# A cross network on one core: a new table of row products, from a planner whose model has the ring's banks, the kernel's order of reads, close input tiles and longer phases

## The chip, the cores and the metric

The kernel runs on one NeuronCore of a Trainium2 chip. The metric is the device time of one execution, in microseconds. Five engines take part, each with a queue of its own that it works through in order: PE (TensorE, the matmuls, with its weight loads shown as PEld), ACT (ScalarE), DVE (VectorE), POOL (GpSimd) and SP (SyncE, which here only issues DMAs). They wait for each other through semaphores. PSUM, into which PE writes, has eight banks of 512 columns; one bank holds one result of 128 features by 512 batch rows.

## The reference: what is computed

Six cross layers over a batch of 16384 rows with 416 features, in bfloat16:

```python
x = x0
for l in range(6):
    proj = x @ ws[l] + bs[l]        # [16384, 416] x [416, 416]
    x = x0 * proj + x
```

Layer l+1 needs the whole feature vector of layer l, but only of its own batch rows, so different parts of the batch are independent of each other.

## The kernel before, in words

**Tiling.** The batch is cut into 8 groups of 2048 rows; a pair (g, l) is a job, group g at layer l, and there are 48 jobs. x lies transposed in SBUF, features on partitions. The 416 features make three full tiles of 128 (NT = 3) and a tail of 32. A group has 4 chunks of 512 columns (NJ = 4). The tails of the four chunks lie stacked in one 128-partition tile, 32 partitions each (`x3s`), so that chunk j of a job has its tail in row quarter `quad(g, l, j)`.

For one chunk of one output tile of a job, PE must add 13 products of 32 contraction rows: each of the three full tiles gives four (one for each 32-row quarter of the array), and the tail gives one, on the row quarter in which it lies. A "row product" is a 32x128 weight against a 32x512 moving operand, placed at one of the array's four row groups. The four row groups run side by side, each into a different PSUM bank; two row groups must not write the same bank at the same time.

**Order of the jobs.** Jobs run along diagonals of (group, layer) (`order`), so that a job's input was made by a job a few places earlier. The output tiles of most jobs form one list of chunks, 504 of them, from tile 1 of job (0, 2) to tile 0 of job (7, 4): the stream (`stream`). The 32-feature output tails of the jobs are computed apart from it, in 14 phases that fall between chunks, each for three jobs (`tails`). A phase uses column groups of the array instead of row groups: 36 products of 128x32 (L694) and 12 of 32x32 (L682) into three banks.

**The table.** The order of the row products on PE is written out by hand in the string `ORDER`, the result of a search outside of the kernel. Each letter is a visit of one row to one chunk: with k the letter's place in the alphabet `LETTERS`, the row is k mod 4 and the chunk is the one begun k div 4 chunks before the next new one; k div 4 = 0 (A to D) begins the next chunk. A visit issues all that this row has to do for this chunk: three products, and a fourth on the row that holds the tail (for the last four chunks of the stream, the tail's product alone). A bar `|` is a phase. There are 2018 visits and 14 bars.

**The planner.** `replay` walks the table and gives every product a time on a clock of its own, 20 units (`SLOT`) to a product. That clock decides three things and then is gone: the order in which the products of the four rows are interleaved in PE's single queue (`out.sort`), the PSUM bank of each chunk (the bank that comes free first on that clock), and, through `read`, when DVE's work for a chunk is put behind a phase's own DVE work (`behind_tail`). In the clock:

- a row that goes to a chunk another row has just left waits `FENCE` units after that row's last product;
- when all four rows are done with a chunk, ACT reads its bank `READ` units later, ACT takes `NEXT` units a read, and the bank is free `BACK` units after the read's start (`over`);
- a phase of m jobs takes all rows off for 65 m + 27 units and uses three free banks;
- at the stream's start, banks 0 to 3 are free, 4 and 5 come free at 92, 6 and 7 at 186, and ACT is busy until 170.

The chip takes no notice of this clock. On the chip PE issues the products in program order and stops at the first one whose bank has not been read by ACT or whose input has not been written by DVE.

**After PE.** When a chunk's 13th product is issued in the program, `evacuate_chunk` adds ACT's eviction with the bias (L547, PSUM to `tw`), and for each pair of chunks of a tile DVE's multiplication with x0 (L559) and the addition of x (L564), which writes the tile that the next layer reads. The eviction frees the bank. ACT evicts in the order in which the last products are issued. The phases' results go through ACT (L605) or DVE (L601), and DVE (L607, L609); in some jobs SP then rotates the stacked tail by whole quarters with two DMAs (L441, L442).

**Before and after the stream** whole tiles are computed with 128-row matmuls (L647, L635, L668), and their banks come from `ring`, a list of the eight bank numbers from which `take` removes the first n and puts them at the end. The tile just before the stream is tile 0 of job (0, 2); ACT evicts it with two reads of 1024 columns (L511). After the stream, `ring` is set from the banks that are left.

**SP's queue** holds the loads of the groups in the order in which the program adds them: `start_job` adds the load of a group's x0 when the first product of a certain job is added (that of group 4 with job (2, 1), whose first chunk is number 56 of the stream), and `tails` adds rotations and outputs when a phase is added.

Of the kernel before, what the change touches and what calls it, by code (L numbers as in the profile page):

```python
# [21 lines left out]
class Program:  # L22
# [175 lines left out]


SLOT = 20  # L200
FENCE, CHANGE = 22, 9
READ, NEXT, BACK, SECOND, PAIR, TAILS = 19, 56, 70, 92, 56, 220
LETTERS = "ABCDEFGHIJKLMNOPQRSTUVWXYZabcdefghijklmnopqrstuvwxyz0123456789"
ORDER = (
    "ABCDABaXOTUBCjUReLMhSHIVOTYBOIDhKAbJCQLVOEBXOQDNKADZOQXBOIDVCfMJSXYFOIDVCMXdSIHB|CXMRCPIBaDUZKTA"
    "JaTMVCLUBSXANSLUdCLMVTCNISDYJSPEBCTAZSPUJGDQVCTIBaTJAKDcZWTAJOTUZKHQBCXQNKDIZSDQJCTANSbAZSLUBKTU"
    "NCLAZWTMBKPcVSDIR|CTJUCTIVODANaTUJGDAZSXINCLUBSXANSLgVGPAVODUNKDUJCXIRCDUNSbAJCTUZLMeRXCINSDYJSP"
    "EBCTAZSPUJGDQVCTANaTUJCDUZOTEBaPURCLQNCbMBWPIZSDIR|CTJUCTIVCDUNaTIBaTVAKTNUGDMVSDINCXANCbVgSLENW"
    "DUNCPUJSDIRObEBCTUBSPAZCTUZKDUJaDIRWPEZKTMBKDRcLCIRCnJQCDMVaTIFWPQBCTMVCPAZWPIBWDUNCPcVKTEZOXANW"
    "QBP|QBOLRECTBCUPZSAPRaXASJPUBKUPRCAPRWYDSJMXCJUDSJMXGBAbWdAXORLUCJTUOBLUCVTMCJDQaVLMCXBQOXJEaBDU"  # L210
    "OZTEKVDUKTBQKNDICbRICTBYSPBMaLVAKTVAKPQVGDcNWDUN|ICXJTACVQPCNAPeVAPeRYLWNQDKNbCIBWTYBSLMVCLMVCXM"
    "JSDIZSPFACTUBSPIVCDYVOTANaTAZKTUNGDNUSDJAXCMVSDgJSbUFLOAVDOQVCPQJCfIRODJAaDMVKDcJSbAJTOYVGDMVCjU"
    "N|ISDJTAKRATBODUeNTYGVATVOIDJWAXRKDYBWPQBObRCQDdOQLVaMDWJMTCJAfSVIDSJUDRKUPFCMDBaQfVKALRWMDJOUDV"
    "CMTBOYjREWDRWMLBUKDVISNXACBSYXJOEDaVDQBSbcJOXEZCXM|RCPISFDAWTcBKTMVGDUNSDMJTCIBSXIdOHQBPCMVDOAZW"
    "PBUOLAVCfURCTcJWPQZCPIRWDJQWPEBCTAZSPUJCLAZCXMRaLUBWLAVLSgNXGIRCDUNS|IDJTECRODANCfYVKTMFWDUNCPAN"
    "aXJQODdATOJUCLUBSXANKDYVCPQhaXFICXRYCPIRWDJQWDAVOTBMKbAVCPcRWLYFCXQZCPIRWDJQWPEBCTAZSPUJCLAZCXMR"
    "aLUBWLAVLSgNXGIRCDUNS|IDJTECRODANCfYVKTMFWDUNCPANaXJQODdATOJUCLURODINCbUBWTMJCLAZWTANSLUBDSUhLYN"
    "GXIRCTBMSBPIaRDICTVICBXcaRPEWDNQWLBQKDZICbRAaTJUOHBMWRDICXRYKPBAaPRWAPRKUDJCYTCNYDWZMLeBUbKRMHWB"
    "MXRCM|RCPISFDAWDMVKTYFCDYROfIFCXQZKDRIeDQJPGABfQVKHMBWPAOVAPKVADNWTYJGDYBWTMZKXEBWDQVOLAVKTAJSAD"
    "OVYDNKYTBKbMVSHBeMXRCM|RCPISFDQCDMVaTIBSbUBTKMVCLMVSDIBSXIZDKURDSMJCbIBSXIZOHQBCTMVCPIVSDQJCTIBa"  # L220
    "DUZSLAJbQOVHAOBbUOBLUChTIVOALVOQDJCXQBiLMSVDKMBbWJMHCVASXdIDJSUPCJUDSVIDSBMbRCYLRCQbJWALVMSDJMaD"
    "JYOXRAO|ANXKQBLSABOXYRGLMVDWNACbNAaXNSDYNSDYJCTUCfVISbENWLBUSDAVOTYJGDQVODINDCNYXSEBSjMVGLQBSDMR"
    "KDAdOXBUOLAVCfURCTcJWPQZCPIRWDJQWPEBCTAZSPUJCLAZCXMRaLUBWLAVLSgNXGIRCDUNS|IDJTAKRMDJCQbJWATVCQPJ"
    "WALBaUTBODUadTIGVATVOIDJWAXRKYPFCMDBaMTCZAPVaIDJSAfRKUPFCMXBWgLROEDNmAXJOQDJCQXKxEPBWMDNWAPVKAXB"
    "OQDNaAPZKcTFODMZWDUJOfAVK|MBXKNALWNQCDNQCbJAWTBQePVGbARWPYCPJUSFDQCTIZCTANaDYVKPQFWDAVMKbRUTBSNM"
    "CD"
)


def replay(tails, events, keep, part):  # L230

    n = len(tails)
    size = [[(3 if c < n - keep else part) + (r == tails[c]) for r in range(4)] for c in range(n)]
    free, flight, begun, act = [0] * 4, {}, 0, 170
    banks = [(0, 0), (0, 1), (0, 2), (0, 3), (92, 4), (92, 5), (186, 6), (186, 7)]
    home, read, out, latest, due = {}, {}, [], [[]] * 4, list(events)

    def over(now):
        nonlocal act
        for end, c in sorted((end, c) for c, (left, end, q) in flight.items() if not left and end <= now):
            del flight[c]  # L250
            if c < n - keep:
                start = max(act, end + READ)
                act, read[c] = start + NEXT, start + BACK
                banks.append((start + BACK, home[c]))
        banks.sort()

    for letter in ORDER:
        if letter == "|":
            now, m = min(free), due.pop(0)
            parts = [(f - now) // SLOT for f in free]  # L260
            at = now + max((f - now) % SLOT for f in free)
            over(at)
            on = at + 65 * m + 3 * CHANGE
            moved = [on + SLOT * k for k in parts]
            for f in flight.values():
                f[1] = moved[f[2]] if f[1] == free[f[2]] else -9 * SLOT
            got = [banks.pop(0) for _ in range(m)]
            assert all(t <= at + 3 * SLOT * k for k, (t, _) in enumerate(got))
            for r in range(4):
                for k in range(parts[r]):  # L270
                    latest[r][-1 - k][0] = moved[r] - SLOT * (k + 1)
            for k, (_, b) in enumerate(got):
                if k == 1:
                    banks.append((on + SECOND, b))
                    continue
                start = max(act, on - CHANGE + READ)
                act = start + NEXT
                banks.append((start + BACK, b))
            banks.sort()
            free = moved  # L280
            out.append([at, -1, [b for _, b in got], on])
            continue
        age, r = divmod(LETTERS.index(letter), 4)
        c, now = begun - age, free[r]
        over(now)
        if not age:
            t, home[c] = banks.pop(0)
            start, begun = max(now, t), begun + 1
            flight[c] = [sum(1 << q for q in range(4) if size[c][q]), 0, r]
        else:  # L290
            start = max(now, flight[c][1] + FENCE)
        assert flight[c][0] >> r & 1
        free[r] = start + SLOT * size[c][r]
        flight[c] = [flight[c][0] & ~(1 << r), free[r], r]
        latest[r] = [[start + SLOT * k, r, c, home[c]] for k in range(size[c][r])]
        out += latest[r]
    over(max(free))
    assert begun == n and not flight and not due
    out.sort(key=lambda x: (x[0], x[1]))
    return out, read, [b for t, b in banks]  # L300


def bass_standalone__cross_network_dcn__recsys_kernel(
# [8 lines left out]
    NT = 3  # L312
    NJ = 4
# [61 lines left out]
    ring = list(range(8))  # L375
# [56 lines left out]
    def turn_of(g, l):  # L432
        return (0, 1, 1, 2)[g % 4] if l % 2 else 0

    def quad(g, l, j):
        q = (j + turn_of(g, l)) % NJ
        return q, slice(q * T32, (q + 1) * T32)
# [417 lines left out]
    def job_banks():  # L855
        return take(NJ)
# [3 lines left out]
    x0n7, x5n, on = (x0s[s][:, 0:XW + CH].rearrange(view, j=NJ, k=KK) for s in (sn, s5, so))  # L860
# [75 lines left out]
    tiles = [((1, 0), 0), ((1, 0), 1), ((0, 1), 0), ((0, 1), 1), ((0, 1), 2), ((1, 0), 2)]  # L936
# [12 lines left out]
    k = 0  # L949
# [52 lines left out]
    def stream(run, keep, part):  # L1002

        chunks = [(it[1], it[2], j) for it in run if it[0] == "tile" for j in range(NJ)]
        due, n = [], 0
        for it in run:
            if it[0] == "tails":
                due.append((n, it[1]))
            else:
                n += NJ  # L1010
        plan, read, left = replay([quad(g, l, j)[0] for (g, l), i, j in chunks], [len(b) for n, b in due],
                                  keep, part)
        phases.extend(on for _, r, _, on in plan if r < 0)
        count, seen = {}, {}
        for _, r, c, b in plan:
# [8 lines left out]
            q, ecols = slice(r * T32, (r + 1) * T32), slice(i * P, (i + 1) * P)  # L1024
            t = seen[c, r] = seen.get((c, r), -1) + 1
# [16 lines left out]
        banks = [home[c] for c in range(len(chunks) - keep, len(chunks))]  # L1042
# [25 lines left out]
    for n, it in enumerate(items):  # L1068
        if n == s_lo:
            stream(items[s_lo:s_hi], NJ, 0)  # L1070
# [15 lines left out]
        elif mode[n] in ("FR", "F1"):  # L1086
            banks = job_banks()
# [3 lines left out]
        else:  # L1091
            banks = job_banks()
# [13 lines left out]
    g, l = LAST, L - 1  # L1106
# [113 lines left out]
    for kk in range(1, KK):  # L1220
        begun = (1,) if kk == 1 else ()
# [47 lines left out]
```

## Time and profile before

| | us |
|---|---|
| median of 3 runs | 470.0 (469.94 to 470.43) |
| the profiled execution, whole | 470.27 |
| its span, first to last instruction | 468.5 |
| PE busy | 460.2 |
| DVE busy | 402.9 |
| ACT busy | 379.1 |
| the stream, first row product to the next full product after it | 40.86 to 432.34 |
| first column product of the phases 1, 2, 3 | 56.11, 81.65, 106.66 |
| the same of the phases 13 and 14 | 387.40, 416.39 |

The granted TensorE clock is full (0.999). In a row of the cost groups stand the line of the code, the engine, what is written and read, the shape, the count, the busy time and the mean duration of one in ns, and after the second bar the time that the engine stood idle just before such instructions and what ended it. A matmul's duration reaches to the end of its way through the array, so that matmuls that follow each other overlap; how fast they follow is read from their starts. In the chain, consecutive pieces of one kind are joined, with their number behind an x. In a line of waits stand the waiting engine with its line, what it waited for, the total in us, the number of times and the longest.

### The profile page before, as it was taken

How to read it: one execution, taken by the hardware profiler on the slowest of the kernel's cores; microseconds unless marked ns; L12 is line 12 of the kernel's file. 1: busy time of each engine (PE TensorE's matmuls, PEld its weight loads, DVE VectorE, ACT ScalarE, POOL GpSimd, SP SyncE). 2: the span in 40 equal slices, each digit the busy share in tenths (PEclk: the TensorE clock that was granted, in tenths of full speed). 3: DMA queues.
4: the chain of work that ended last, by engine and by line, in shares of the span. 5: the costliest groups of instructions: out<-in, count | busy, mean ns of one | idle time of the engine just before them, and what ended most of it. 6: DMA issues, size and time to landing. Idle time of an engine off the chain costs nothing.

```text
span 468.5 us, 17458 instructions
## 1 busy us (share of the span) xinstructions
PE 460.2 (98%) x7827; PEld 259.6 (55%) x7833; DVE 402.9 (86%) x700; ACT 379.1 (81%) x605; POOL 7.6 (2%) x15
## 2 busy tenths in 40 slices
PE   9999999999999999999999999999999999999995
PEld 5344555565556666575555556565576564545442
DVE  1897898898899898989899899898989889789897
ACT  4686898888888798888878888888887888878685
POOL 1000000000000000000000000000000010000000
PEclk9999999999999999999999999999999999999999
DMA  8986750480002879094848447990100195025999
GB/s 221 191 150 138 169 122 13 81 138 25 3 3 36 149 202 160 26 148 148 160 81 146 148 82 137 160 298 19 25 2 6 35 159 158 3 46 108 240 192 261
DMA packets 139087, 53.77 MB, mean 115 GB/s; under 512 B 112762, under 2 KB 138500, under 8 KB 139012
## 3 DMA queue, kind: packets, MB, share of 16 engines
q1 hardware_dynamic: 138856, 52.54, 53.5%
q8 instruction: 61, 1.00, 0.9%
q10 hardware_dynamic: 156, 0.11, 0.1%
q14 instruction: 14, 0.11, 0.1%
HBM read 5.97 MB, written 13.63 MB: 42 GB/s over the span
## 4 chain that ended last, share of the span: by engine, by line
PE 94%; DVE 3%; DMA 1%; ACT 1%; issue 0%; DVEq 0%; ACTq 0%
PE ps L1030 69%; PE ps L694 7%; PE ps L1034 6%; PE ps L647 6%; PE ps L635 2%; PE ps L682 1%; DMA x<-x 1%; DVE x L1184 1%; PE ps L768 1%; PE ps L668 1%; DVE x L1178 1%; PE ps L786 1%; ACT tw L511 1%; DVE x L525 0%; DVE tw L520 0%
## 5 line engine op out<-in xcount | busy, mean ns | idle before, releaser
L1030 PE MATMUL ps<-x,wm 32*128 32x512 bf16 x6000 | 357.0, 374 | 1.5 <-DVE x L564 1.0
L547 ACT ACTIVATE tw<-ps,bias 128x512 bf16<-128x512 f32 x500 | 311.1, 688 | 48.0 <-PE ps L1030 38.0
L1030 PEld LDWEIGHTS ps<-x,wm 32*128 32x128 bf16 x6000 | 208.3, 92 | 134.3 <-ACT tw L547 3.2
L559 DVE TENSOR_TENSOR tw<-tw,x 128x1024 bf16<-128x1024 bf16 x250 | 168.3, 689 | 44.5 <-ACT tw L547 44.0
L564 DVE TENSOR_TENSOR x<-tw,x 128x1024 bf16<-128x1024 bf16 x250 | 163.5, 688 | 0.5
L1034 PE MATMUL ps<-x,w 32*128 32x512 bf16 x504 | 149.1, 374 | 0.0
L1034 PEld LDWEIGHTS ps<-x,w 32*128 32x128 bf16 x504 | 41.7, 92 | 6.8 <-issue 0.2
L511 ACT ACTIVATE tw<-ps,bias 128x512 bf16<-128x512 f32 (+1 forms) x43 | 34.7, 879 | 12.5 <-PE ps L668 8.1
L647 PE MATMUL ps<-x,wm 128*128 128x512 bf16 x146 | 33.8, 382 | 0.9 <-issue 0.8
L694 PE MATMUL ps<-x,wm 128*32 128x512 bf16 x564 | 33.6, 380 | 0.0
L605 ACT ACTIVATE ts<-ps,bias 128x512 bf16<-128x512 f32 x33 | 21.0, 687 | 15.1 <-PE ps L682 15.1
L520 DVE TENSOR_TENSOR tw<-tw,x 128x1024 bf16<-128x1024 bf16 (+1 forms) x35 | 21.6, 628 | 4.9 <-ACT tw L511 4.6
L647 PEld LDWEIGHTS ps<-x,wm 128*128 128x128 bf16 x152 | 14.0, 98 | 18.9 <-issue 3.4
L694 PEld LDWEIGHTS ps<-x,wm 128*32 128x32 bf16 x564 | 13.5, 96 | 18.6 <-ACT tw L547 3.8
L525 DVE TENSOR_TENSOR x<-tw,x 128x1024 bf16<-128x1024 bf16 (+1 forms) x35 | 20.6, 624 | 0.0
L609 DVE TENSOR_TENSOR x<-ts,x 128x512 bf16<-128x512 bf16 x47 | 18.4, 420 | 0.4
L607 DVE TENSOR_TENSOR ts<-ts,x 128x512 bf16<-128x512 bf16 x33 | 13.0, 419 | 0.0
L906 POOL COPY ost<-ot 128x512 bf16<-128x512 bf16 x6 | 6.1, 1022 | 413.3 <-DMA ot<-x 413.3
L601 DVE SCALAR_TENSOR_TENSOR ts<-ps,bias,x 128x512 bf16<-128x512 f32 x14 | 10.5, 747 | 1.1 <-PE ps L682 1.0
L1120 PE MATMUL ps<-wm,x 128*128 128x416 bf16 x48 | 9.8, 340 | 0.1
L1172 ACT ACTIVATE x<-ps 128x416 bf16<-128x416 f32 x16 | 7.6, 518 | 2.4 <-PE ps L1120 2.4
L796 DVE COPY x<-ps 128x512 bf16<-128x512 bf16 x5 | 2.0, 423 | 8.6 <-PE ps L786 8.6
(50 smaller groups left out, 76.8 us busy)
## 6 DMA issues: line engine op xcount, KB each, us to landing
out_dram<-ost SPq DMA_DIRECT2D x6, 1664.0 KB, 7.1
x<-x SPq DMA_DIRECT2D x24, 96.0 KB, 2.3
x<-in_x_dram SPq DMA_DIRECT2D x8, 208.0 KB, 4.2
x<-in_x_dram SPq DMA_DIRECT2D x4, 416.0 KB, 7.9
out_dram<-ost SPq DMA_DIRECT2D x2, 832.0 KB, 6.7
wm<-in_ws_dram SPq DMA_DIRECT2D x5, 312.0 KB, 3.3
x<-x SPq DMA_DIRECT2D x22, 64.0 KB, 2.0
out_dram<-x SPq DMA_DIRECT2D x3, 416.0 KB, 4.6
```

The costliest lines, as they stand in the source:

```text
L511: add("act", lambda h, a=a, w=w, b0=b0: h.activation(tw[r][:, a * CH:(a + w) * CH], psum[:, b0 * CH:(b0 + w) * CH], ACT_F.Identity, bias=b ...
L520: add("dve", lambda h, a=a, e=e: h.tensor_tensor(tw[r][:, a * CH:e * CH], tw[r][:, a * CH:e * CH], x0s[s0][:, i * GC + a * CH:i * GC + e * ...
L525: add("dve", lambda h, a=a, e=e: h.tensor_tensor(xs[so][:, i * GC + a * CH:i * GC + e * CH], tw[r][:, a * CH:e * CH], src(i, a, e), ALU.ad ...
L547: add("act", lambda h: h.activation(tw[r][:, j * CH:(j + 1) * CH], bank(b), ACT_F.Identity, bias=bias[:, i, l:l + 1], scale=1.0), reads=[( ...
L559: add("dve", lambda h: h.tensor_tensor(tw[r][:, o], tw[r][:, o], x0s[s0][:, c], ALU.mult), reads=[("tw", r, k) for k in both] + [x0_tok(s0 ...
L564: add("dve", lambda h: h.tensor_tensor(xs[so][:, c], tw[r][:, o], src(i, a, a + 2), ALU.add), reads=[("tw", r, k) for k in both] + [stok(i ...
L605: add("act", lambda h: h.activation(ts[r][:, :], bank(b), ACT_F.Identity, bias=bias[:, 3, l:l + 1], scale=1.0), reads=[("ps", b), "bias"], ...
L609: add("dve", lambda h: h.tensor_tensor(x3s[so][:, :], ts[r][:, :], res, ALU.add), reads=[("ts", r)] + rtok, writes=[("x3", so), ("x3", so, ...
L647: add("pe", lambda h, t=t, j=j, k=k, w=w: h.matmul(bank(banks[j])[:, k * w:(k + 1) * w], wm[l][:, t, ecols], src(t, j, j + 1)[:, k * w:(k ...
L694: add("pe", lambda h, t=t, j=j, src=src, l=l, b=b, ro=ro, qo=qo: h.matmul(psum[qo, b * CH:(b + 1) * CH], wm[l][:, t, NT * P:D], src(t, j, ...
L1030: add("pe", lambda h, l=l, t=t, j=j, b=b, q=q, ecols=ecols, src=src, kw=kw: h.matmul(bank(b), wm[l][q, t, ecols], src(t, j, j + 1)[q, :], ...
L1034: add("pe", lambda h, l=l, b=b, q=q, ecols=ecols, s3=s3, kw=kw: h.matmul(bank(b), w3[l][q, ecols], s3[q, :], **kw), reads=tok3 + [("w3", l ...
```

## The change

Only the table, the planner's model and the way its bank numbers are used are changed. No line that issues an instruction is touched.

- **Table.** `ORDER` is replaced by another string, again with 2018 visits and 14 bars. 22, 60, 86, 122, 157, 193, 229, 257, 293, 333, 365, 409, 449 and 485 chunks have been begun when the phases come; before, the second came at 54 and the tenth at 337, the others at the same numbers.
- **Banks of the ring.** `replay` still counts banks from 0 to 7, but its numbers are now places in `ring` as it stands at the stream's start, and `stream` turns them into bank numbers.
- **Start.** ACT is taken to be busy until 156 units, and the last four banks to come free at 84 and 178.
- **Order of reads.** Chunks that end in the same slot are read by ACT in the order of the rows that end them, and no longer in that of their numbers.
- **Close input tiles.** A chunk whose input tile is made by chunks less than 30 places earlier begins no earlier on the clock than `SUMS` = 240 units after those chunks' banks come free (`read`), less a slot for each product that comes before that tile's.
- **Longer phases.** A phase takes 60 m + 52 units: 232 for three jobs, where it was 222.

```diff
-FENCE, CHANGE = 22, 9
-READ, NEXT, BACK, SECOND, PAIR, TAILS = 19, 56, 70, 92, 56, 220
+FENCE, PHASE, CHANGE = 22, 52, 9
+READ, NEXT, BACK, SECOND, PAIR, TAILS, SUMS = 19, 56, 70, 92, 56, 220, 240
 ORDER = (
-    "ABCDABaXOTUBCjUReLMhSHIVOTYBOIDhKAbJCQLVOEBXOQDNKADZOQXBOIDVCfMJSXYFOIDVCMXdSIHB|CXMRCPIBaDUZKTA"
+    "ABCDAJCXaFTMWDUNSLYBKTMZjGANDaMpCPUJCXIROEDBaTUJCITVCQLVCAXNaALVaQHNKUTBQKDRICbRK|AJDWQJDCfUNSDM"
...
-    "WALBaUTBODUadTIGVATVOIDJWAXRKYPFCMDBaMTCZAPVaIDJSAfRKUPFCMXBWgLROEDNmAXJOQDJCXQKxEPBWMDNWAPVKAXB"
-    "OQDNaAPZKcTFODMZWDUJOfAVK|MBXKNALWNQCDNQCbJAWTBQePVGbARWPYCPJUSFDQCTIZCTANaDYVKPQFWDAVMKbRUTBSNM"
+    "WALBaUTBODUadTIGVATVOIDJWAXRKYPFCMDBaMTCZMLRWALRCAfROUDJeUTaBQPKVEDVSMDJOAfJCQXKZMDJWATJWMDVKMTB"
+    "CARaXMBKPZUDWRIPaAJbCYVTO|EJDWQBPCNAbOVLQCJDUiRLaAJbSUNDKMXCBMTWJYHOAVPCMVDOUBPWIRDIORXENKLAUKBN"
     "CD"
 )
-def replay(tails, events, keep, part):
+def replay(tails, events, needs, keep, part):
...
-    free, flight, begun, act = [0] * 4, {}, 0, 170
-    banks = [(0, 0), (0, 1), (0, 2), (0, 3), (92, 4), (92, 5), (186, 6), (186, 7)]
+    free, flight, begun, act = [0] * 4, {}, 0, 156
+    banks = [(0, 0), (0, 1), (0, 2), (0, 3), (84, 4), (84, 5), (178, 6), (178, 7)]
...
-        for end, c in sorted((end, c) for c, (left, end, q) in flight.items() if not left and end <= now):
+        for end, q, c in sorted((end, q, c) for c, (left, end, q) in flight.items() if not left and end <= now):
...
-            on = at + 65 * m + 3 * CHANGE
+            on = at + 3 * SLOT * m + PHASE
...
             start, begun = max(now, t), begun + 1
+            for t, d in needs[c]:
+                start = max([start] + [read[d + k] + SUMS - SLOT * t for k in range(4)])
...
+        tiles = [it[1:] for it in run if it[0] == "tile"]
+        place = {it: NJ * k for k, it in enumerate(tiles)}
+        needs = [[(t, place[(g, l - 1), t]) for t in range(NT if c < len(chunks) - keep else part)
+                  if c - place.get(((g, l - 1), t), -99) < 30] for c, ((g, l), i, j) in enumerate(chunks)]
         plan, read, left = replay([quad(g, l, j)[0] for (g, l), i, j in chunks], [len(b) for n, b in due],
-                                  keep, part)
+                                  needs, keep, part)
+        at = list(ring)
+        plan = [(t, r, c, at[b]) if r >= 0 else (t, r, [at[k] for k in c], b) for t, r, c, b in plan]
+        left = [at[k] for k in left]
```

More of the change, by code (lines that the diff above doesn't have):

```diff
@@ L200 @@
 SLOT = 20
-FENCE, CHANGE = 22, 9
-READ, NEXT, BACK, SECOND, PAIR, TAILS = 19, 56, 70, 92, 56, 220
+FENCE, PHASE, CHANGE = 22, 52, 9
+READ, NEXT, BACK, SECOND, PAIR, TAILS, SUMS = 19, 56, 70, 92, 56, 220, 240
 LETTERS = "ABCDEFGHIJKLMNOPQRSTUVWXYZabcdefghijklmnopqrstuvwxyz0123456789"
 ORDER = (
-    "ABCDABaXOTUBCjUReLMhSHIVOTYBOIDhKAbJCQLVOEBXOQDNKADZOQXBOIDVCfMJSXYFOIDVCMXdSIHB|CXMRCPIBaDUZKTA"
[L206 to L224, printed above, removed]
-    "OQDNaAPZKcTFODMZWDUJOfAVK|MBXKNALWNQCDNQCbJAWTBQePVGbARWPYCPJUSFDQCTIZCTANaDYVKPQFWDAVMKbRUTBSNM"
@@ new lines @@
+    "ABCDAJCXaFTMWDUNSLYBKTMZjGANDaMpCPUJCXIROEDBaTUJCITVCQLVCAXNaALVaQHNKUTBQKDRICbRK|AJDWQJDCfUNSDM"
+    "dSbJECbURCTINWDUJSPAJCTAZSPUJCDVYOTJAaDYVKTENCbNUSDJAXSYJGPAVODNUDOJUTCIRCDUNSbAJTaMVKHQBCXQNCPI"
+    "ZSDJQCDMVaTEJOXBUDOAZXOIRGDYBSXARLOYBXKMZG|QBPSIVDCPAZOXQJGDQBaTINCLAdSXJYOHRACTNUCPJUSDAVCXRMaL"
+    "FUCXARWPYBKPAdaLUNCLMVTCNISDcBWPIRCLAVSbMBKPYVSHMB|CTMVCPIVCDUNaTIBaTVAKTNUGDMVSDINCXYJCDMVSbIFW"
+    "PQBCTMVCPIVSDIBWTANKTYVODAZOTUJGDURODINCbUJODBMSbIVCTUBSPIVGDQVCTMJWDAZSXINGDUBSXIBKTAZKPcRGAZPW"
@@ new lines @@
+    "QBP|QBOLRECTBCUPZSAPRaXASJPUBKUDVSAPRKAbSNcDOUbFKDURKDIRCbQJOXBIODVAOTUJCLQVCDUNSbEJWDQVCTINCbUJ"
+    "ODIBaTVAKTNUGDMVSDINCXBcXSNAKPAZWLAVKTYNGDYNSDYN|ICXJTACVQPCNAPeVAPeRYLWNQDKNbCIBWTYBSLMVCLMVCXM"
+    "JSDAdWPQBLOQBbKNQCDdMWTZEODNUKTABOXAVCTcVOLERCDcRaPAJWbMRKHYBCXQNCPIZSDJQCDMVaDMJSbAJTOYVGDMVCjU"
+    "N|ISDJTAKRMDJCQDNeITVGMbBWIDRWIDRKAbJSMDBObQJCDdOQXJaMDJWMTBKAXhSMDJOUDVKQPFCMDBaQfVKALRWMDJOUDV"
+    "KATBOYjREWDROULBKUTBSIBLCUdCMLZSAbJSUDRKMXeFLQBCXMR|CPISFDQCTIBaDUZKDQJWbMBXOIZCLQBSbIdODIVCTUJO"
@@ new lines @@
+    "DIVODIBbCNYXKERDCUdTaIBTaJUOHAVCTMVKDUJSDAVCXQNKDYJWfAJWTMZGDMVCXcNS|IDJTECRCTANaDYVKTMFWDUBOXAN"
+    "KXZQODZATOJUCLURODINCbIBWTJYOHAVCTMVKDUJSDIRDCUNSbBISbVAKPURCLMRWDINCXIBWTJgOHAVCTMVKDUJSDAVCXQN"
+    "KDYJSfAJaPURGDMdCbUN|ISDJTECRCTANaDMVKTFYWDAVOTYJGXAVODNUDOJUTCIRODIBSbUJPCIVDQCZTMBaLMBaXIBWLQZ"
+    "ODIZCXQZKPAJWDRMWDNUKTBISBDUORbAOZDaULNQGXJCQXBAWPRaIDRKUDJSUPGBAbVCMDVOYLFSUPBeMXRCM|RCPISFDQCT"
+    "IBaTIVOHQBPCMVDOAZWPBUOLQBCfURODIdWPQZGDQNCbINWDINXGQBPAWBQPKVDIVSPAJODYJCXQKZPEBWDQNWLAVKTAJSAD"
@@ new lines @@
+    "OVYDNKTYBKbMVSHBeMXRCM|RCPISFDQCDMVaTIBSbUBTKMVCLMVSDIBSXIZDKURDSMJCbIBSXIZOHQBCTMVCPIVSDQJCTIBa"
+    "DUZSLAJbQOVHAOBbUOBLUChTIVOALVOQDJCXQBiLMSVDKMBbWJMHCVASXdIDJSUPCJUDSVIDSBMbRCMLRCcbJOALVMaDJMaD"
+    "JYOXRAO|ANXKQBLSABOXYRGLMVDWNACbNQWDNISDJAWfBcSXJMGbVQCPRCPISFDAeTUBKTMVCLUNSDMJTCIBWTIdOHQBPCMV"
+    "DOAZWPBUKDQVCfIRWPYFCXQZCPIRWDJQWPEBCTAZSPUJCLAZCXMRaLUBWLAVLSgNXGIRCDUNS|IDJTAKRMDJCQbJWATVCQPJ"
+    "WALBaUTBODUadTIGVATVOIDJWAXRKYPFCMDBaMTCZMLRWALRCAfROUDJeUTaBQPKVEDVSMDJOAfJCQXKZMDJWATJWMDVKMTB"
```

## The prediction

> **What bounds the kernel now.** I read the page's busy shares and chain first, then its cost groups, then the stretches between phases in the windows view, then the waits, timeline and chain around the two stretches that stand out.
>
> ```profile
> PE 460.2 (98%) x7827; PEld 259.6 (55%) x7833; DVE 402.9 (86%) x700; ACT 379.1 (81%) x605; POOL 7.6 (2%) x15
> ...
> PE 94%; DVE 3%; DMA 1%; ACT 1%; issue 0%; DVEq 0%; ACTq 0%
> ...
> L1030 PE MATMUL ps<-x,wm 32*128 32x512 bf16 x6000 | 357.0, 374 | 1.5 <-DVE x L564 1.0
> L547 ACT ACTIVATE tw<-ps,bias 128x512 bf16<-128x512 f32 x500 | 311.1, 688 | 48.0 <-PE ps L1030 38.0
> ```
>
> TensorE is the bound, but its busy time hides the loss: four row groups run side by side, so PE is "busy" while a row stands empty. The pace is read from starts instead. The chain view has a dense run of eleven full products:
>
> ```profile
> 432.34 2.54 PE ps L647 x11
> 435.20 5.29 PE ps L647 x24
> ```
>
> The last lasts 0.38 (its row on the page), so ten steps take 2.16 us: 0.2158 us a slot, and four row products share one, 0.054 us each. The stream's 6504 products need 350.9 us at that pace. It runs from 40.86 to 432.34, cut by 14 phases. Windows from phase to phase:
>
> ```profile
> 40.86:56.11 15.25, 14.80 (x262) 1.00 0.56 124
> 56.11:81.65 25.54, 25.49 (x468) 1.00 0.36 79
> 81.65:106.66 25.01, 25.01 (x468) 1.00 0.61 103
> 189.54:217.39 27.85, 27.85 (x520) 1.00 0.63 135
> 300.86:323.26 22.40, 22.40 (x416) 1.00 0.66 190
> 387.40:416.39 28.99, 28.03 (x522) 1.00 0.29 72
> 416.39:432.34 15.95, 15.79 (x276) 1.00 0.41 76
> ```
>
> Columns: stretch, length, PE busy and its matmuls, clock, DMA share and rate. A count holds the phase's 48 products and four to six still running at its left edge: 416 row products in the second and third line, 468 in the fourth and sixth. Take 0.054 a product off and the third and fourth both leave 2.57-2.60 us: the price of one phase and its changes of form. The thirteen stretches that begin with a phase and end with one leave 2.57 to 2.76, except the second line (3.10) and the sixth (3.74). So nearly all loss sits in four places: the start, 0.53 us in the second line (25.54 - 25.01, equal counts), 1.14 us in the sixth (28.99 - 27.85, equal counts), and the last line, 15.95 - 228 x 0.054 = 3.65, which is 1.1 over the usual 2.57 and shows no wait.
>
> The start, as timelines of PE and ACT; the waits in the second line's stretch at 65.5 to 67 and 73 to 76; the chain in the sixth:
>
> ```profile
> 40.86 0.39 PE L1030 MATMUL ps<-x,wm 32*128 32x512 bf16 x3
> 41.70 0.82 PE L1030 MATMUL ps<-x,wm 32*128 32x512 bf16 x9 [0.45 <-ACT tw L511]
> ...
> 40.53 2.12 ACT L511 ACTIVATE tw<-ps,bias 128x1024 bf16<-128x1024 f32 x2 [0.16 <-PE ps L647]
> ...
> PEld ps L1030 <- ACT tw L547: 0.3, 1, 0.3
> ...
> PEld ps L1030 <- ACT tw L547: 0.7, 2, 0.5
> ...
> 408.39 1.27 ACT tw L547 x2
> ...
> 410.38 1.22 DVE x L564 x2
> 411.60 0.05 issue
> 411.64 0.39 PE ps L1030 x4
> ```
>
> **The change part by part.** No instruction is added or removed by it: both tables have 2018 visits and 14 bars, 504 chunks and the same products. What changes is the order on PE, and which PSUM bank a chunk gets. The longer phase (3 x 20 x 3 + 52 = 232 units for 222) and the initial times are clocks of the planner; the chip's phase stays 2.57, so they cost nothing by themselves and act only through the table.
>
> *Banks by the ring.* Taking banks off the ring call by call up to the stream gives 7, 0, 1, 2, 3, 4, 5, 6, and the tile before the stream sits in 3 to 6. The old kernel uses the planner's numbers raw, so its fourth chunk lands in bank 3. ACT's two double evictions free 3 and 4 at 41.6 and 5 and 6 at 42.65; PE issues three products at 40.86 and stands until 41.70. The new kernel maps its first four chunks to 7, 0, 1, 2, all free: sixteen products, 0.86 us, which end as 3 and 4 come free. Bounds: the idle shown, 0.45, and both stops in full, 0.84 and the 0.33 between the last products before 42.70 and the loads that come back then. I take 0.75, nearest to the first stop: rows must still change chunk there.
>
> *Order of reads.* Following the old table's letters, two pairs of chunks end in one slot: 25 on row 0 with 23 on row 1, then 37 on row 0 with 36 on row 1. The old sort frees the lower chunk first; the program issues row 0 first, so ACT reads 25 and 37 first, and the bank promised first comes one eviction (0.69) late. The trace has these last products near 64.1 and 72.8, and the loads wait for ACT right behind, near 66 and 74. The new sort, by end and then row, is the kernel's. Gain: the 0.53 of equal counts (0.3 to 1.0 by the wait lines). Next late there is nothing that this view shows.
>
> *Input tiles that lie close.* In the old table chunk 478 reads tile 2 of (7,2) only 45 products after the last product of chunks 462 and 463, which make it. The chain shows the way from there: 408.31 (the last product) to ACT x2, DVE, PE at 411.64: 3.33 us, 62 products. 17 short are 0.92 us; the idle reads 0.96. In the new table the smallest such distance is 133 products, 7.2 us, so this wait goes with 3.9 us to spare. Gain 1.14. At worst the hold comes back as empty rows in the order: gain nil.
>
> *The new order itself.* It rewrites nearly every stretch (only the twelfth keeps 172 of 176 letters). What it leaves empty I can bound only by rows: wait-free stretches lie 0 to 0.19 above 2.57, on average 0.04, and the last 1.1 above. I charge 0.08 for the two mended stretches and 0.15 for the start: 0.23. Bounds: -1.0 if the last stretch were mended, +1.5 if ten others came out like the worst wait-free one.
>
> *What moves with it.* The second phase comes after 60 chunks begun, not 54, and the tenth after 333, not 337. Chunk 56 starts (2,1), whose load of group 4 (four transposing DMAs and four copies, SP 88.78 to 102.72) now stands ahead of that phase's four rotations on SP's queue. SP is idle from 70.60, so the load issues then, to about 84.5; the rotations wait for the phase's DVE sums until about 90, land by about 95, and the next phase needs them at about 105. Cost nil; cover 10 us. No POOL or ACT queue entry changes place by it except evictions, which follow the products.
>
> Sum: 0.75 + 0.53 + 1.14 - 0.23 = 2.2 us off the profiled execution's 470.27 (span 468.5 and 1.8 around it), so 468.1. The median of the runs shown is 0.27 below that execution: 467.8.
>
> **A rule against it.** The row gives 0.2158 us a slot. "TensorE: Matmul & The Clock Gate" of the Trainium skill, section "Back-to-back issue gap", puts a sustained stream of loads and 512-column matmuls at about 131 ns each. By that the stream would need about 213 us of PE (an estimate from that page), ACT would be the bound, and taking waits off PE would give nothing. The trace disagrees, at 215.8, and the measurement decides.
>
> **The rivals.**
> - *Hold written into the order.* The planner can only keep chunk 478 back if older chunks fill the rows; with eight banks it may have left them empty. Then the 1.14 and part of the start stay: 470.0 - 0.53 - 0.5 = 469.0. For it: the last stretch already loses 1.1 without a wait. Against: the other wait-free ones lose next to nothing.
> - *Slower: banks run short elsewhere.* Every rewritten stretch is a new chance for a load to wait for ACT, at 0.53 a stretch as at 56 to 81. It decides from about six of fourteen; with seven, 470.0 - 2.2 + 3.7 = 471.5. Against: ACT is idle 48 us before its evictions, mostly for PE's products, and counting products from the eighth-last finished chunk to each new one, the tightest is 2.75 slots in the old table and 3.75 in the new.
> - *ACT sets the pace, not PE.* The evictions' 311 us lie in a stream of 391, and holds on PE are then hidden: 470.0. Against: equal counts differ by just the wait (1.14 against 0.96 idle and its restart). The rule above would end here.
>
> **How the numbers follow.** Forecast 0.72 (its own range 466.8 to 468.4, from the bounds of start and order), hold in the order 0.16, banks short 0.08, ACT's pace 0.04. Within 0.2%, 0.94 us, this kernel cannot be told from no change. Faster: 0.70 of the first and half of the second, 0.78. Same: 0.02 + 0.08 + 0.04 = 0.14. Slower: 0.08. The range of 8 in 10, 466.8 to 469.6, holds the forecast and most of the second case and leaves out the slower one, no change, and the tail below.
>
> **What would show it.** The fourth row product at once after 40.86 and no idle for ACT L511; phases one to three 49.85 us apart, not 50.55; thirteenth stretch near 27.8 with no idle for DVE x L564; all others still 2.57 to 2.76 over their products. Wrong, if a new idle of PE for L547 or L564 above 0.3 us appears, or stretches without a wait come out above 2.8.

## The result

The new kernel takes 467.5 us (median of four runs, 467.31 to 467.64) against 470.22 of the old one beside it: a ratio of 0.9941, 95% interval 0.9924 to 0.9958. The forecast was 467.8. The profiled execution's span fell from 468.5 to 465.7.

The page of the new kernel, busy shares, chain, and the groups of row products and their evictions (code lines are ten, or three, higher: L1040 was L1030, L550 was L547):

```profile
PE 458.9 (99%) x7827; PEld 263.8 (57%) x7833; DVE 404.2 (87%) x700; ACT 379.1 (81%) x608; POOL 6.8 (1%) x15
...
PE 93%; DVE 4%; DMA 1%; issue 1%; ACT 0%; SPq 0%; DVEq 0%
...
L1040 PE MATMUL ps<-x,wm 32*128 32x512 bf16 x6000 | 356.0, 374 | 0.0
L550 ACT ACTIVATE tw<-ps,bias 128x512 bf16<-128x512 f32 x500 | 310.5, 688 | 46.4 <-PE ps L1040 35.9
```

The row products' idle of 1.5 us, for DVE and for ACT, is gone, and the busy times have hardly moved. ACT counts three instructions more (608 for 605): behind the stream other banks are left over, three pairs of them no longer lie side by side, and each such pair is read by two instructions instead of one. Again the stretches say more. The windows of the new kernel's stream, PE alone, same columns as before. Stretch n is here the one that begins with phase n; shown are the start, the stretches 1, 2, 6 and 13, and the last (14):

```profile
40.74:55.28 14.54, 14.54 (x266) 1.00 0.69 133
55.28:84.41 29.13, 29.13 (x544) 1.00 0.70 142
84.41:105.11 20.70, 20.70 (x389) 1.00 0.05 15
187.94:216.05 28.11, 28.11 (x521) 1.00 0.59 129
385.89:413.77 27.88, 27.88 (x522) 1.00 0.30 78
413.77:429.67 15.90, 15.75 (x277) 1.00 0.48 101
```

The row products in them are 261, 492, 336, 468, 468 and 228. At 0.054 us each the start leaves 0.46 where it left 1.39; stretches 1 and 2 leave 2.59 and 2.57 where they left 3.10 and 2.57; stretch 13 leaves 2.63 where it left 3.74. Stretch 6 has become longer with the same 468 products: 28.11 for 27.85, and between 201 and 211 us loads wait there for ACT:

```profile
PEld ps L1040 <- ACT tw L550: 0.6, 2, 0.4
```

From its first row product to the full product after it the stream takes 388.93 us for 391.48, 2.55 less. (Both streams are written one slot, 0.22 us, too long, for a reason that the last section gives; the difference stands.) Of the span's other 0.2 us about 0.1 lies ahead of the stream and 0.1 behind it, where PE's order was not changed.

The start, as PE's timeline in the new kernel. All sixteen products of the first four chunks are issued without a stop, where the old kernel stood after three:

```profile
40.74 0.83 PE L1040 MATMUL ps<-x,wm 32*128 32x512 bf16 x12
41.40 0.38 PE L1044 MATMUL ps<-x,w 32*128 32x512 bf16 x4
41.61 1.06 PE L1040 MATMUL ps<-x,wm 32*128 32x512 bf16 x12
```

### The profile page after: what moved, and what is told of

The parts are those of the page before. It is cut to its first block, busy times and chain, and to the rows that moved or that the text cites. A ratio compares the mean times of both kernels' runs of the same rounds, so it can differ in the third digit from the quotient of the medians.

```text
span 465.7 us, 17469 instructions
## 1 busy us (share of the span) xinstructions
PE 458.9 (99%) x7827; PEld 263.8 (57%) x7833; DVE 404.2 (87%) x700; ACT 379.1 (81%) x608; POOL 6.8 (1%) x15
## 4 chain that ended last, share of the span: by engine, by line
PE 93%; DVE 4%; DMA 1%; issue 1%; ACT 0%; SPq 0%; DVEq 0%
PE ps L1040 70%; PE ps L697 7%; PE ps L1044 6%; PE ps L650 6%; PE ps L638 2%; PE ps L685 1%; DMA wm<-in_ws_dram 1%; DVE x L1194 1%; DVE x L1188 1%; DVE x L528 1%; DVE tw L523 1%; PE ps L671 1%; ACT tw L514 0%; PE ps L789 0%; SPq L734 0%
## 5 line engine op out<-in xcount | busy, mean ns | idle before, releaser
L1040 PE MATMUL ps<-x,wm 32*128 32x512 bf16 x6000 | 356.0, 374 | 0.0
L550 ACT ACTIVATE tw<-ps,bias 128x512 bf16<-128x512 f32 x500 | 310.5, 688 | 46.4 <-PE ps L1040 35.9
L1040 PEld LDWEIGHTS ps<-x,wm 32*128 32x128 bf16 x6000 | 212.5, 92 | 127.7 <-ACT tw L550 4.1
L1044 PE MATMUL ps<-x,w 32*128 32x512 bf16 x504 | 151.7, 374 | 0.0
L1044 PEld LDWEIGHTS ps<-x,w 32*128 32x128 bf16 x504 | 42.7, 92 | 6.6
```

Of the source, the lines that this page charges most:

```text
L550: add("act", lambda h: h.activation(tw[r][:, j * CH:(j + 1) * CH], bank(b), ACT_F.Identity, bias=bias[:, i, l:l + 1], scale=1.0), reads=[( ...
L1040: add("pe", lambda h, l=l, t=t, j=j, b=b, q=q, ecols=ecols, src=src, kw=kw: h.matmul(bank(b), wm[l][q, t, ecols], src(t, j, j + 1)[q, :], ...
L1044: add("pe", lambda h, l=l, b=b, q=q, ecols=ecols, s3=s3, kw=kw: h.matmul(bank(b), w3[l][q, ecols], s3[q, :], **kw), reads=tok3 + [("w3", l ...
```

## The experiments

Some facts about the program itself, read by following each table with the one or the other rule, set what is worth a run. Of a table's 2018 letters 14 are the bars, so there are 2004 visits. With the new table, the old phase length, the old order of reads, or no rule for close tiles give the very same products in the same order and the same banks, to the last one. So in the new kernel these three act only through the table that was made with them. The old start times are another matter: with them 16 products at the start change places. With the old table the new order of reads changes banks but no place in the queue, and the tile rule changes the place of 66 products. The two tables often stand in the same state at the same letter, so that one can be continued with the other.

Three theories were held against rivals: that the start's loss was a wrong bank, that of stretch 1 a bank promised too early, that of stretch 13 a tile read too soon. (The expectations call stretch 1 also the second stretch, the start being the first.)

**Only the ring's banks, with the old table.**

```diff
         plan, read, left = replay(...)
+        at = list(ring)
+        plan = [(t, r, c, at[b]) if r >= 0 else (t, r, [at[k] for k in c], b) for t, r, c, b in plan]
+        left = [at[k] for k in left]
```

> The old table and the old model; only the bank numbers go through the ring (7, 0, 1, 2, 3, 4, 5, 6), so the fourth chunk starts in a free bank. Theory (the start's loss is a wrong bank): the stop after the first three row products goes, the first stretch shrinks from 15.25 us by 0.75 to 0.95, all other stretches stay (25.54 for the one after phase 1, 28.99 for the thirteenth); 0.8 us off the kernel. Rival (the new table's other first letters do it): the first stretch keeps 15.2 us and the time stays at 470.

Measured: 469.26 us, ratio 0.9983 (0.9973 to 0.9992). Windows of this kernel, the start and the stretches 1 and 13:

```profile
40.84:55.33 14.49, 14.49 (x262) 1.00 0.58 128
55.33:80.87 25.54, 25.49 (x469) 1.00 0.44 79
386.64:415.62 28.98, 28.02 (x520) 1.00 0.28 71
```

The start lost 15.25 - 14.49 = 0.76 us and the two other stretches kept their length. The theory holds.

**Only the new order of reads, with the old table.**

```diff
-        for end, c in sorted((end, c) for c, (left, end, q) in flight.items() if not left and end <= now):
+        for end, q, c in sorted((end, q, c) for c, (left, end, q) in flight.items() if not left and end <= now):
```

> The old table; of the model only the order in which two chunks that end in one slot are read. The order of the products is the old one to the last, banks differ from chunk 23 on. Theory (a bank promised one eviction too early): the stretch after phase 1 shrinks from 25.54 to 25.0 us and the loads' waits for ACT near 66 and 74 us go; the start (15.25) and the thirteenth stretch (28.99) stay; 0.5 us off. Rival (the new order around there did it): 25.5 us stays, and the time with it.

Measured: 469.32 us, ratio 0.9979 (0.997 to 0.9989). The same three windows:

```profile
40.44:55.68 15.24, 14.79 (x262) 1.00 0.72 142
55.68:80.70 25.02, 25.02 (x469) 1.00 0.30 68
386.31:415.30 28.99, 28.03 (x522) 1.00 0.29 71
```

Stretch 1 lost 0.52 us without one product changing its place. Loads' waits for ACT between 64.5 and 75.5 us fall from 1.1 us in three to 0.2 in one. The first chunk that gets another bank is number 32: it takes the bank of chunk 25, which ACT reads first, and no longer that of 23. The theory holds; the rewritten order there was not needed. The time fell by 0.9 us, more than this stretch; 0.15 of it is stretch 10, which varies by itself (last section).

**Only the end of the new table, behind the old one.**

```diff
-ORDER = old
+ORDER = old[:1865] + new[1865:]
```

> The old kernel with the new table's letters from place 1865 on (chunk 466 and later), nothing else. The two tables stand in the same state there, so only the end is new. Theory (distance of 42 products between the last product of chunk 463 and the first product that reads its tile, now 126): the thirteenth stretch falls from 28.99 to 27.8 to 27.9, with no idle of PE for DVE's addition; start and second stretch keep 15.25 and 25.54; 1.1 us off. Rival (it is DVE's backlog or a bank, which the rest of the new order cured): most of the 1.1 us wait stays.

Measured: 468.94 us, ratio 0.9979 (0.9969 to 0.9988). The same windows:

```profile
40.47:55.72 15.25, 14.80 (x262) 1.00 0.65 128
55.72:81.25 25.53, 25.48 (x468) 1.00 0.35 75
387.02:414.83 27.81, 27.81 (x520) 1.00 0.29 76
```

Stretch 13 lost 1.18 us, the others shown nothing; in this kernel's groups the row products wait for ACT alone (0.5 us, the start). The theory holds.

**The new kernel with raw bank numbers.**

```diff
-        at = list(ring)
-        plan = [(t, r, c, at[b]) if r >= 0 else (t, r, [at[k] for k in c], b) for t, r, c, b in plan]
-        left = [at[k] for k in left]
```

> The new kernel, with the planner's bank numbers used raw as before. Theory: the first stretch grows by 0.75 to 0.95 us from 14.54 (261 products), PE stops after three row products until ACT's first double eviction ends; everything else as in the new kernel; 0.8 us slower than it. Rival (the new first letters cured the start): 14.5 us stays.

Measured: 468.3 us, ratio to the old kernel 0.9962 (0.9947 to 0.9977). The start's window, then PE's timeline there:

```profile
40.45:55.92 15.47, 15.02 (x266) 1.00 0.58 123
```

```profile
40.45 0.39 PE L1037 MATMUL ps<-x,wm 32*128 32x512 bf16 x3
41.30 0.82 PE L1037 MATMUL ps<-x,wm 32*128 32x512 bf16 x9 [0.45 <-ACT tw L514]
```

The old stop is back with its 0.45 of idle, and the start costs 0.93 us more than in the new kernel. So the mapping is needed for the whole of the start's gain, and it is worth more with the new first letters (0.93) than with the old ones (0.76): they leave 0.46 over the products' pace, where the old ones with the right banks leave 0.62. With the new letters came the planner's new start times, and no run separates the two.

**Only the tile rule, with the old table.**

```diff
             start, begun = max(now, t), begun + 1
+            for t, d in needs[c]:
+                start = max([start] + [read[d + k] + SUMS - SLOT * t for k in range(4)])
```

> The old table; of the model only the rule that a chunk begins no earlier than its close input tile allows. It changes the place of 66 products in the queue and no letter. The first product that reads the late pair then stands 31 products behind the last product of chunk 463 (chunk 479), where it was 42 (chunk 478). Theory (only a table made with the rule helps; PE waits for what is missing to some 62 products): the wait grows from 1.0 to about 1.6 us, the thirteenth stretch from 28.99 to about 29.5. Rival (the rule itself moves other products ahead and cures the wait): the thirteenth stretch falls towards 27.9.

Measured: 471.4 us, slower than the old kernel, ratio 1.0027 (1.0017 to 1.0038). The window of stretch 13, then PE's timeline around the wait:

```profile
386.95:417.20 30.25, 29.50 (x520) 1.00 0.27 69
```

```profile
407.86 2.58 PE L1037 MATMUL ps<-x,wm 32*128 32x512 bf16 x29
411.19 0.39 PE L1037 MATMUL ps<-x,wm 32*128 32x512 bf16 x3 [0.74 <-DVE x L567]
```

The direction is the theory's, the size is not: 30.25 against 29.5 expected. PE's full stop is even shorter (0.74 for 0.96). The rest is rows that stand empty while PE counts as busy, ahead of the stop and again behind it: between 407.86 and 410.1 only 29 products start, where 2.2 us hold 41. Matched to the queue, row 3 starts nothing from 408.10 to 409.84: its next product is chunk 476's, which the planner's clock now holds back, and everything that stands behind it in PE's single queue keeps that place. The rule alone does not make the wait go; a held chunk needs a table that puts other work in its place.

**The late visit moved.** The late visit is the last one of chunk 463, on row 1, twelve chunks after the chunk was begun. One kernel has it one visit of its row earlier, one has it two earlier.

```diff
-    ...XBWgLROEDNmAXJOQDJCQXKxEPBW...
+    ...XBWgLROEDNmAXJOQDtCQXKNEPBW...      (one visit earlier)
+    ...XBWgLROEDNmAXpOQDNCQXKNEPBW...      (two visits earlier)
```

> The old kernel with one exchange in its table: the late last visit of chunk 463 on row 1 changes places with the visit before it on that row. Distance 54 products instead of 42. Theory (the way from the last product over ACT and DVE's two operations takes 3.33 us, 62 products): PE's idle for DVE's addition falls from 0.96 to about 0.4 us; the exchange may leave rows empty, by the planner some 0.4 us, so that the stretch is 28.4 to 28.9. Rival (the wait is DVE's backlog of other pairs): the idle stays near 1.0.

> As the single exchange, with the visit moved two places earlier: distance 66 products. Theory: PE does not stop for DVE's addition at all (at most 0.1 us); the stretch still pays for empty rows, 27.9 to 28.6. Rival (DVE's backlog): an idle of over 0.5 us stays.

Measured: 470.15 us, ratio 0.9999 (0.999 to 1.0008), and 469.85 us, ratio 0.9994 (0.9985 to 1.0003). The group of row products of the kernel with one exchange, its stretch 13, and stretch 13 of the other:

```profile
L1030 PE MATMUL ps<-x,wm 32*128 32x512 bf16 x6000 | 357.3, 374 | 1.0 <-DVE x L564 0.5 <-ACT tw L511 0.5
```

```profile
386.91:415.83 28.92, 28.44 (x520) 1.00 0.28 71
```

```profile
387.30:415.83 28.53, 28.53 (x521) 1.00 0.29 73
```

Counted in PE's queue the distances are 42, 54 and 66 products, and the idle for DVE's addition is 0.96, 0.5 and nothing. So the distance decides whether PE stops: one visit that is moved takes the stop away, with the rest of the old order in place. It is not shown that the way is a fixed 62 products, nor that it is free of other pairs' work. From the start of chunk 463's last product to the end of the addition that completes its tile, the traces have 3.46 us in the old kernel, 3.85 with one exchange, 3.16 with two, and 3.03 in the new kernel. DVE's timeline with one exchange shows why:

```profile
408.12 1.29 DVE L559 TENSOR_TENSOR tw<-tw,x 128x1024 bf16<-128x1024 bf16 x2
409.32 1.28 DVE L564 TENSOR_TENSOR x<-tw,x 128x1024 bf16<-128x1024 bf16 x2
```

In each line the first operation is another pair's, and only the second is the late pair's; DVE has no idle there from 405.10 on. In the old kernel another pair's addition (0.6 us) stands ahead too. So DVE's work for other pairs, the rival, is a part of the way, though not the whole of the wait. The stretch itself recovers only 0.07 and 0.46 of the 1.18: with two exchanges each row stands empty for some 0.7 us, though PE no longer stops.

**Three repairs and the rest of the old table.** The old letters up to place 1865, the new ones behind, the ring's banks and the new order of reads; phases, start times as before, no tile rule.

```diff
-ORDER = old
+ORDER = old[:1865] + new[1865:]
-        for end, c in sorted((end, c) for c, (left, end, q) in flight.items() if not left and end <= now):
+        for end, q, c in sorted((end, q, c) for c, (left, end, q) in flight.items() if not left and end <= now):
+        at = list(ring)
...
```

> The old table up to place 1865 and the new one behind it, with the ring's banks and the new order of reads; the old phases, the old start times and no rule for input tiles. Theory (three repairs are all of it): first stretch 14.42, the one after phase 1 25.01, the thirteenth 27.81, the stream 389.0 us long against 388.94 in the new kernel, and the same time within 0.3 us (467.5 to 467.8). Rival (rewriting the other stretches brought something as well): the stream stays above 389.4 and the time above 467.9.

Measured: 467.37 us (467.1 to 468.16), ratio 0.9939 (0.9925 to 0.9953): the new kernel's time. The same three windows:

```profile
40.66:55.15 14.49, 14.49 (x262) 1.00 0.61 129
55.15:80.17 25.02, 25.02 (x469) 1.00 0.37 81
385.93:413.74 27.81, 27.81 (x521) 1.00 0.29 75
```

The stream takes 388.76 us; without the slot that is written too much, the new kernel's takes 388.71 and the old one's 391.26. The three repairs add up (0.76 + 0.52 + 1.18 = 2.46, against 2.50) and are the whole of the gain; rewriting the other stretches brought nothing that can be measured.

**Against the new wait.** In stretch 6 of the new kernel loads wait for ACT near 203 and 210 us. Two kernels put old letters back there.

```diff
-ORDER = new
+ORDER = new[:675] + old[675:1063] + new[1063:]
```

> The new kernel with the old table's letters between two places where the tables stand in the same state (675 to 1063: the sixth, seventh and eighth stretch or so). In the new kernel the stretch from 187.87 to 215.98 us has a wait for ACT near 203 us and is 0.25 longer than the old one with the same 468 products. Theory (that wait comes of the new letters there): that stretch falls from 28.11 to 27.85, nothing else changes, 0.25 us off the time, hardly to be told by the clock alone. Rival (the banks that the stretch inherits make it): a wait of 0.2 us or more stays.

```diff
-ORDER = new
+ORDER = new[:778] + old[778:882] + new[882:]
```

> The new kernel with the old letters between places 778 and 882 only, where the new table waits for ACT near 203 and 210 us. Theory: those waits go (28.10 to 27.86 in that stretch), and with the new letters kept elsewhere no other stretch grows by more than 0.05; 467.2 to 467.3. Rival (a bank order that is passed on makes waits elsewhere): another stretch gives 0.1 us or more back.

Measured: 467.44 us, ratio 0.9944 (0.9931 to 0.9957), and 467.23 us, ratio 0.9936 (0.9923 to 0.9949). Windows of the first of them, stretches 6 and 11, then stretch 6 of the second:

```profile
187.70:215.56 27.86, 27.86 (x521) 1.00 0.68 131
321.29:354.94 33.65, 33.65 (x624) 1.00 0.04 10
```

```profile
187.94:215.96 28.02, 28.02 (x521) 1.00 0.68 129
```

In the first, the wait is gone (28.11 to 27.86), so it came of the new letters, and the rival fails. But stretch 11, whose letters are those of the new kernel, takes 33.65 for 33.48; the loss is made near 344.6, where a load waits 0.3 us for ACT. Banks that run short because of the splice do not explain it: from chunk 261 on, long before stretch 11, the products have the new kernel's order, and the banks are the new kernel's under other names, one for one. What made ACT late there is open, and 0.17 us is about what stretch 10 varies by between kernels that agree in it (last section).

In the second the loads' waits near 203 and 210 are gone and no other stretch grows, but the stretch falls by 0.09 only. The other 0.16 us stands at its end: in the splice the last slot ahead of the phase holds a product of row 1 alone, and three empty rows are 3 x 0.054 = 0.16. So neither kernel shows a wait that is passed on through the banks, and neither is told from the new kernel by its time.

## Why the prediction was right

**What bounds the kernel.** Right: PE's issue, at 0.054 us a row product, and 2.57 us a phase. In all the kernels run, a stretch from one phase to the next keeps to it within 0.2 us or shows a wait, with one exception: stretch 13 with the visit two places earlier leaves 3.28, for rows that stand empty. The new kernel's dense run of full products after the stream is again 2.54 us for eleven. The rule of the Trainium skill ("TensorE: Matmul & The Clock Gate", "Back-to-back issue gap") that the prediction held against itself spoke for no gain. It is not borne out here: full products still start 0.216 us apart, and each wait taken off PE came off the stream in full.

**Banks by the ring.** Right in place and size: 0.75 foreseen, 0.76 by itself. The 0.15 charged on it was wrong in sign: the new first letters, with their start times, gave 0.17 more, and the start's net gain was 0.93.

**Order of reads.** Right: 0.53 foreseen, 0.52 by itself, with the order of products untouched. In the whole old table only the two pairs named there end in one slot and are read in the wrong order, so they were the cause.

**Close input tiles.** Right: 1.14 foreseen, 1.11 in the new kernel and 1.18 with the new end alone. That the tile was read too soon was confirmed by moving the visit. The working behind it was looser than its result. The distances of 45 and 133 were counted in the table's letters; in the queue they are 42 and 126, so that the 17 missing products (0.92 us) came so near the idle's 0.96 was partly luck. And the chain's 3.33 us are not the way of chunk 463 alone: its last product starts at 408.12, the first of the two evictions is chunk 470's, and the first of the two additions is another pair's. Its worst case, the hold written into the order, did not come in the new table, but it exists: it is what the rule did to the old table (1.3 us slower).

**The new order itself.** The term was charged with 0.23, and that the whole came near it is luck. The two mended stretches cost 0.02 and 0.06 over nothing, as charged; the start cost nothing; stretch 6 has a new wait of 0.26, which was not foreseen; and stretch 10 leaves 2.58 where it left 2.76, which was not foreseen either. The wait in stretch 6 is the mechanism of the slower rival, banks that run short elsewhere, in one stretch instead of seven. The last stretch kept its loss: it leaves 3.60 now and left 3.65, of which 0.22 is the slot written too much, so that it lies 0.9 over 2.57 and not 1.1.

**What moves with it.** Right: the load of group 4 is issued from 68.69 us, ahead of the second phase's rotations, which follow at 88.18; the stretch that holds the load has 2.59 and the next 2.57. That no instruction is added holds for PE and DVE; ACT has its three more reads behind the stream, and the span takes no longer there (36.03 us for 36.12).

**The sum.** 2.2 us foreseen, 2.55 measured in the stream; the start makes up nearly all of the difference. Phases one to three are 49.83 us apart, where 49.85 was written. One of the signs was not met: stretch 6 leaves 2.86 over its products, where every other stretch was to stay within 2.76. It does so with waits of loads, the longest 0.4 us, while PE itself shows no idle there.

## What to carry to other kernels

When an order is planned ahead, look for the places where the plan's clock and the machine part: equal work between two marks that takes unequal time shows them at once, even where the engine counts as busy. Three small errors of the plan (which bank is free, who is read first in a tie, how long a result takes to come back) were the whole of what the new kernel gained, and mending those at their places was worth as much as planning everything anew. A constraint that is added to a plan without planning anew can cost more than the wait that it describes, because every later product keeps its place in the queue: here the rule alone made the kernel 1.3 us slower.

## What the runs showed of the hardware that was not expected

The same instructions take the same time to a hundredth of a microsecond in most stretches of different kernels (stretch 3 takes 27.82 us for 468 products in every one), yet not in all: stretch 10 of the old order came out at 22.40, 22.31 and 22.25 us in kernels that agree in it to the last product. The loss is one event near 304.4 us. In the old kernel a load waits there for DVE's read of a phase's result:

```profile
PEld ps L1030 <- DVE ts L601: 0.3, 1, 0.3
```

DVE ends this read 3.63 us after the phase's first product in the kernels with 22.40, 3.54 in the one with 22.31, and 3.32 in the kernel with the tile rule alone, which has 22.25 and no such wait. Why DVE comes to it earlier or later is open. A difference of 0.15 us in one stretch of one profile is therefore no evidence of an effect of the change.

A record that is missing can look like a wait. At the stream's end the profiles of the old and the new kernel show 0.16 us of issue time ahead of the first full product, and the other profiles show none. In the old kernel's groups there are six matmuls fewer than weight loads of the full products; the kernel with the new end alone has 152 of both:

```profile
L647 PE MATMUL ps<-x,wm 128*128 128x512 bf16 x146 | 33.8, 382 | 0.9 <-issue 0.8
L647 PEld LDWEIGHTS ps<-x,wm 128*128 128x128 bf16 x152 | 14.0, 98 | 18.9 <-issue 3.4 <-ACT x L798 0.6 <-ACT tw L511 0.2
```

One of the six is the first full product behind the stream: the dense run has eleven matmuls of 2.54 us in these two profiles, and twelve of 2.70 in the others. So the last windows of the two, 15.95 and 15.90 us, hold one slot too much, 0.22 us, and the stretch takes about 15.7 us in both, as in the other kernels.
